# Two-layer token mixer and MLP on one core: x2 loaded between the halves of w1, tile 1 normalised before tile 2's statistics, tile 2 turned after tile 1's product

## The chip, the cores and the metric

The kernel runs on one NeuronCore of one Trainium2 chip. The metric is device time in microseconds (us) of one execution. The kernel before takes 135.35 us, the median of 3 runs (135.31 to 135.44).

## What is computed

All tensors are bfloat16; S = 2048 tokens, D = 512, F = 1792.

```python
h = gelu(layernorm(x) @ w1)                 # w1: 512 x 512
g0..g3 = the four 128-column quarters of h, shifted by +1, -1, +2, -2 tokens, zeros at the ends
x1 = x + concat(g0, g1, g2, g3) @ w2        # w2: 512 x 512
out = x1 + gelu(layernorm(x1) @ w3) @ w4    # w3: 512 x 1792, w4: 1792 x 512
```

`layernorm` subtracts the mean of a token's 512 values and divides by the square root of their variance plus 1e-5; it has no gain and no bias.

## The kernel before, in words

The tokens are cut into 16 tiles of 128. A tile of layer 1 passes these steps, each an operation with a name that carries the tile's number. The line is the one under which the profile lists it.

- `dma_x` (L384) loads x; `dma_w` (L393) loads a weight or half of one. All loads are issued by SP, on one queue, in the order of LOADS.
- Statistics: `bnst` and `bnag` on DVE (L432, L434), or, for the tiles in STAT_ACT (tile 0 among them), `sum` and `ssq` on ACT (L411, L416) followed by the small `msq` and `vpe` on DVE (L424, L428). `rstd` is a power of -0.5 on POOL (L439).
- `norm` (L461 on DVE) writes the normalised tile. Tile 0 is only centred (`norm0_0`, `norm0_1`, L448), and its factor `rstd0` is applied later.
- `tp` (L506) turns the tile on PE, in four 128x128 transposes into PSUM. `ev` (L514) copies the result to xnT in SBUF, on ACT, DVE, or half and half (`ev1act`, `ev1dve`).
- `up1:g` (L642) is the product with w1 in 128-column pieces, 16 matmuls for a group of one tile. Tile 0 uses `rows0` (L544) instead, with tokens as rows: four matmuls of 512 columns, then `gelur0` (L585, ACT, scaled by rstd0), then `th0` (L610, four transposes on PE) and `evh0` (L620, copy on DVE). For the other tiles `gelu1` (L657, ACT) writes h.
- `mix` (L697) is the shifted product with w2, four matmuls of 512 columns. mix0 needs h of tiles 0 and 1, so `evh0` and `gelu1` of tile 1. It is split in two halves. `x1` (L709, L713, DVE) adds x.

Layer 2 normalises x1 the same way, turns most tiles by DMA (L479), and multiplies by w3 (`up2`, L642) and w4 (`down`, L731). `res` (L739, DVE) adds x1, and an output DMA (L742) stores it.

Each engine carries out its own instructions strictly in their order in the program, and waits on semaphores for the results of other engines. PE's order is written out in SCRIPT: `sa`/`sb` are the halves of tile 0's transposes, `ty` a transpose, `ra`/`rb` the halves of rows0. The orders of the other four engines come from a planner (`order` and `place`, L54 to L273) that estimates durations and due times. The order that results for the first tiles is:

- SP: x0-1, x2, w1a, w1b, x3, x4-5, w2b, w2a, x6, ...
- DVE: bnst1, bnag1, norm0_0, norm0_1, bnst2, norm1, bnag2, msq0, vpe0, norm2, ev1dve, bnst3, ev2, bnag3, bnst4, evh0, norm3, ...
- ACT: sum0, ssq0, ev0_0, ev0_1, ev1act, gelur0, sum5, gelu1 of tile 1, ...
- POOL: rstd1, rstd2, rstd0, rstd3, ...
- PE: nine matmuls on zeros (L756), tp0, tp1, rows0, tp2, up1 of tile 1, th0, up1 of tile 2, mix0, tp3, mix1, ...

PSUM has three pairs of banks for `tp`, `rows0` and `up`, handed out in PE's order, one after the other in a ring, and two single banks for `mix`, `down` and `th0`.

Of the kernel before, what the change touches and what calls it, by code (L numbers as in the profile page):

```python
# [6 lines left out]
P = 128  # L7
# [7 lines left out]
class Op:  # L15


    def __init__(self, name, eng, fn, reads, writes, dur, queue):
        self.name, self.eng, self.fn = name, eng, fn
        self.reads, self.writes = list(reads), list(writes)  # L20
        self.dur, self.queue = dur, queue
        self.idx = 0
        self.descs = 8.0
        self.prio = 1e9
        self.first = None

class Program:

    HOP = {"pe": 200.0, "dve": 155.0, "act": 220.0, "pool": 120.0, "sp": 70.0}
    LOOK = {"dve": 300.0, "act": 300.0}
    DUE = 179877.0
    BEGIN = {"sp": 30.0, "act": 150.0, "pe": 400.0, "dve": 150.0, "pool": 450.0}
    ENTRY = 1900.0
    COLD, RESTART = 4300.0, 800.0
    RING = 150.0
    LAG = {"load": 750, "tp": 350}

    def __init__(self):  # L40
        self.ops = []
        self.lines = []

    def add(self, eng, name, fn, reads=(), writes=(), dur=100.0, queue=None):
        op = Op(name, eng, fn, reads, writes, dur, queue)
        op.idx = len(self.ops)
        self.ops.append(op)
        return op

    def line(self, names):  # L50

        self.lines.append(list(names))

    def order(self):  # L54
# [25 lines left out]
        order_only = set()  # L80
        for names in self.lines:
            for a, b in zip(names, names[1:]):
                assert named[a].eng == named[b].eng, (a, b)
                order_only.add((named[a].idx, named[b].idx))
        last = None
        pe_pos = 0
        for op in self.ops:
            if op.eng == "pe":
                if last is not None:
                    preds[op.idx].add(last.idx)  # L90
                last = op
                op.prio = pe_pos
                pe_pos += 1
        order_only = {(a, b) for a, b in order_only if a not in preds[b]}
        for a, b in order_only:
            preds[b].add(a)
        succs = [set() for _ in self.ops]
        for i, d in enumerate(preds):
            for j in d:
                succs[j].add(i)  # L100
        left = [len(s) for s in succs]
        stack = [i for i, n in enumerate(left) if n == 0]
        seen = 0
        while stack:
            i = stack.pop()
            seen += 1
            for j in preds[i]:
                if self.ops[j].eng != "pe":
                    self.ops[j].prio = min(self.ops[j].prio, self.ops[i].prio)
                left[j] -= 1  # L110
                if left[j] == 0:
                    stack.append(j)
        assert seen == len(self.ops), "cycle"
        if self.DUE:

            topo, left = [], [len(d) for d in preds]
            stack = [i for i, n in enumerate(left) if n == 0]
            while stack:
                i = stack.pop()
                topo.append(i)  # L120
                for j in succs[i]:
                    left[j] -= 1
                    if left[j] == 0:
                        stack.append(j)
            due, t = {}, self.DUE
            for op in self.ops:
                if op.eng == "pe" and not op.name.startswith("warm"):
                    due[op.idx] = t
                    t += op.dur
            for i in reversed(topo):  # L130
                op = self.ops[i]
                late = due.get(i, 1e9)
                for j in succs[i]:
                    o = self.ops[j]
                    hop = 70.0 if op.queue else (self.HOP[op.eng] if o.eng != op.eng else 120.0)
                    work = (2300.0 if op.queue == "tp" else op.dur + 1850.0) if op.queue else op.dur
                    late = min(late, o.prio - hop - work)
                op.prio = late
        for op in self.ops:
            op.prio += BIAS.get(op.name, 0.0)  # L140
            if op.first is not None:
                op.prio = op.first
        for names in self.lines:
            for a, b in reversed(list(zip(names, names[1:]))):
                named[a].prio = min(named[a].prio, named[b].prio - 1e-3)

        self.preds = preds
        out = self.place(succs, order_only)
        for a, b in order_only:
            preds[b].discard(a)  # L150
        return out

    def place(self, succs, order_only):

        npend = [len(d) for d in self.preds]
        ready = [0.0] * len(self.ops)
        cands = {e: [] for e in ENGINES}
        for op in self.ops:
            if npend[op.idx] == 0:
                cands[op.eng].append(op)  # L160
        free = dict(self.BEGIN)
        rings = {"sp": [], "act": []}
        fed = {}
        clock = moved = last = turned = self.total = 0.0
        out = []

        def finish(limit):
            nonlocal clock
            while True:
                heads = {e: r[0] for e, r in rings.items() if r}  # L170
                if not heads:
                    return None
                live = [e for e in heads if heads[e][0] <= clock]
                later = min([h[0] for h in heads.values() if h[0] > clock], default=1e18)
                if not live:
                    if later > limit:
                        return None
                    clock = later
                    continue
                first = min(live, key=lambda e: heads[e][1])  # L180
                step = heads[first][1] * len(live)
                ends = clock + step <= min(later, limit)
                if not ends:
                    step = min(later, limit) - clock
                for e in live:
                    heads[e][1] -= step / len(live)
                clock += step
                if ends:
                    return rings[first].pop(0)[2]
                if clock >= limit:  # L190
                    return None

        def release(op, o, at):
            npend[o.idx] -= 1
            if at is not None:
                ready[o.idx] = max(ready[o.idx], at)
            if npend[o.idx] == 0:
                cands[o.eng].append(o)

        def land(op):  # L200
            nonlocal moved, last, turned
            if op.queue == "tp":
                turned = max(clock + 500.0, op.start + 2450.0, last + 500.0, turned + 480.0)
                at = turned + self.LAG["tp"]
            elif op.name.startswith("out"):
                at = clock + 300.0
                self.total = max(self.total, at)
            else:
                moved += op.dur
                at = clock + 600.0 + min(600.0, 0.3 * moved) + (600.0 if op.dur > 1400.0 else 0.0)  # L210
                at += 50.0 if moved <= 1200.0 else self.LAG["load"] - 300.0 if moved <= 4000.0 else self.LAG["load"] if moved <= 11000.0 else self.LAG["load"] + 650.0
            if op.queue != "tp":
                last = max(last, at)
            op.landed = at
            for j in succs[op.idx]:
                if (op.idx, j) not in order_only:
                    release(op, self.ops[j], at + 30.0)

        while len(out) < len(self.ops):
            while True:  # L220
                best = None
                for e in ENGINES:
                    if cands[e]:
                        t = max(free[e], min(ready[o.idx] for o in cands[e]))
                        if best is None or t < best[0]:
                            best = (t, e)
                op = finish(best[0] if best else 1e17)
                if op is None:
                    break
                land(op)  # L230
            t, e = best
            look = self.LOOK.get(e, 1.0)
            op = min((o for o in cands[e] if ready[o.idx] <= t + look), key=lambda o: (o.prio, o.idx))
            cands[e].remove(op)
# [674 lines left out]
```

## Time and profile before

| what | value |
|---|---|
| median of 3 runs | 135.35 us (135.31 to 135.44) |
| span of the profiled execution, first to last instruction | 133.7 us |
| median less span | 1.65 us |
| busy DVE, ACT, POOL | 50.9, 56.0, 30.9 us |
| mean granted TensorE clock | 1.000 |
| DMA moved | 12.19 MB |

The page gives the profiled execution's span, but no time that includes what lies around it. The 1.65 us between the span and the median of the runs are taken as the same for both kernels. Times in a timeline count from the start of the span. A timeline line gives start, duration, engine, line, operation, what is written and read, and, in brackets, the idle time before it and what ended it. Several instructions of a kind may share one line (x4), and the duration then runs from the first one's start to the last one's end. Ends on PE are modelled, and an engine can start an instruction shortly before the end of the one before.

### The profile page before, as it was taken

What the parts mean: (1) busy time and instruction counts of PE and PEld (TensorE: products, weight loads), DVE (VectorE), ACT (ScalarE), POOL (GpSimd) and SP (SyncE); (2) the same over time, 40 slices, a digit from 0 to 9 for tenths busy, and PEclk for the clock granted to TensorE, in tenths of its full rate; (3) what the DMA queues carried; (4) which work ended last, traced back from release to release, by engine and by line L of the source; (5) the groups of instructions that cost most, each with busy time, mean ns of one, the idle gap of its engine ahead of it and who ended that gap; (6) DMA issues with size and microseconds to landing.
All of it is one profiled execution on the core that took longest, in us unless ns stands there. A gap on an engine that the chain in (4) does not pass through costs nothing.

```text
span 133.7 us, 2004 instructions
## 1 busy us (share of the span) xinstructions
PE 130.6 (98%) x776; PEld 71.8 (54%) x789; DVE 50.9 (38%) x138; ACT 56.0 (42%) x89; POOL 30.9 (23%) x69
## 2 busy tenths in 40 slices
PE   8999999999999999999999999999999999999994
PEld 3488768874488444444444444444444444444464
DVE  1899998887550830052260003322220000232223
ACT  5699998858657155520025553000006663000000
POOL 2447567696544120012022003100000000000000
PEclk9999999999999999999999999999999999999999
DMA  4999966745442991002211000311111000111112
GB/s 134 329 349 401 237 150 95 83 89 107 98 99 49 295 329 40 0 0 43 77 42 39 0 0 0 78 39 44 39 42 37 0 0 0 39 44 39 39 39 78
DMA packets 21305, 12.19 MB, mean 91 GB/s; under 512 B 13872, under 2 KB 20784, under 8 KB 21296
## 3 DMA queue, kind: packets, MB, share of 16 engines
q1 hardware_dynamic: 20864, 11.93, 32.7%
q10 hardware_dynamic: 432, 0.13, 0.4%
q8 instruction: 6, 0.10, 0.3%
q14 instruction: 3, 0.02, 0.1%
HBM read 6.82 MB, written 2.10 MB: 67 GB/s over the span
## 4 chain that ended last, share of the span: by engine, by line
PE 94%; DMA 2%; DVE 2%; issue 1%; SPq 0%
PE y_ps L642 46%; PE o_ps L731 36%; PE o_ps L697 10%; DMA x_sb<-in_x_dram 2%; PE y_ps L506 1%; DVE st L432 1%; PE y_ps L544 1%; DVE xn_buf L448 0%; DVE xn_buf L461 0%; DVE o_sb L739 0%; PE o_ps L610 0%; DVE mv L434 0%; SPq L894 0%
## 5 line engine op out<-in xcount | busy, mean ns | idle before, releaser
L642 PE MATMUL y_ps<-xnT,w_sb 128*128 128x512 bf16 (+2 forms) x421 | 63.6, 308 | 0.2
L642 PEld LDWEIGHTS y_ps<-xnT,w_sb 128*128 128x128 bf16 x424 | 38.4, 98 | 24.6 <-DVE mv L434 0.2
L731 PE MATMUL o_ps<-w_sb,h2T 128*128 128x512 bf16 (+3 forms) x248 | 48.7, 355 | 0.2
L657 ACT ACTIVATE h2T<-y_ps 128x1024 bf16<-128x1024 f32 (+1 forms) x29 | 28.6, 993 | 47.2 <-PE y_ps L642 47.1
L731 PEld LDWEIGHTS o_ps<-w_sb,h2T 128*128 128x128 bf16 x252 | 23.6, 98 | 25.2
L739 DVE TENSOR_TENSOR o_sb<-o_ps,x_sb 128x512 bf16<-128x512 f32 (+3 forms) x18 | 11.4, 632 | 45.7 <-PE o_ps L731 45.7
L439 POOL TENSOR_TENSOR rstd<-mv,neghalf 128x1 f32<-128x1 f32 x20 | 11.1, 553 | 35.1 <-DVE mv L434 30.1
L697 PE MATMUL o_ps<-w_sb,hT 128*128 128x512 bf16 x58 | 14.8, 379 | 0.3
L432 DVE BATCH_NORM_STATS2 st<-x_sb 128x6 f32<-128x512 bf16 x20 | 13.5, 676 | 2.6 <-DMA x_sb<-in_x_dram 2.5
L713 DVE TENSOR_TENSOR x_sb<-o_ps,x_sb 128x512 bf16<-128x512 f32 x10 | 6.8, 677 | 14.8 <-PE o_ps L697 14.8
L439 POOL TENSOR_TENSOR rstd<-vpe,neghalf 128x1 f32<-128x1 f32 x12 | 6.7, 558 | 15.6 <-DVE vpe L428 15.5
L473 POOL TENSOR_SCALAR xn_buf<-x_sb,rstd,nmr 128x512 bf16<-128x512 bf16 x12 | 9.2, 764 | 1.0 <-DVE nmr L466 0.4
L657 ACT ACTIVATE hT<-y_ps 128x512 bf16<-128x512 f32 (+1 forms) x10 | 8.1, 806 | 3.1 <-PE y_ps L642 2.9
L697 PEld LDWEIGHTS o_ps<-w_sb,hT 128*128 128x128 bf16 x64 | 6.1, 98 | 5.7
L709 DVE SCALAR_TENSOR_TENSOR x_sb<-o_ps,x_sb 128x512 bf16<-128x512 f32 x6 | 4.1, 681 | 12.1 <-PE o_ps L697 12.1
L416 ACT ACTIVATE junk<-x_sb 128x512 bf16<-128x512 bf16 x12 | 7.5, 622 | 2.1 <-DVE x_sb L709 2.0
L461 DVE TENSOR_SCALAR xn_buf<-x_sb,mv,rstd 128x512 bf16<-128x512 bf16 x13 | 6.1, 471 | 2.7 <-POOL rstd L439 2.0
L470 ACT ACTIVATE xn_buf<-x_sb,nmr,rstd 128x512 bf16<-128x512 bf16 x6 | 4.9, 813 | 0.5 <-POOL nmr L466 0.4
L756 PE MATMUL o_ps<-zeros 128*128 128x512 bf16 x9 | 4.0, 631 | 0.4 <-DVE zeros L363 0.4
L411 ACT ACTIVATE junk<-x_sb 128x512 bf16<-128x512 bf16 x6 | 3.7, 624 | 1.2 <-DMA x_sb<-in_x_dram 1.2
L434 DVE BATCH_NORM_AGGREGATE mv<-st 128x2 f32<-128x9 f32 x20 | 3.8, 192 | 0.3
L506 PE MATMUL y_ps<-ident,xn_buf 128*128 128x128 bf16 x32 | 3.4, 236 | 0.2 <-DVE xn_buf L461 0.2
(34 smaller groups left out, 28.7 us busy)
## 6 DMA issues: line engine op xcount, KB each, us to landing
out_dram<-o_sb SPq DMA_DIRECT2D x15, 128.0 KB, 1.7
w_sb<-in_w_dram SPq DMA_DIRECT2D x1, 1792.0 KB, 10.9
w_sb<-in_w_dram SPq DMA_DIRECT2D x2, 896.0 KB, 6.2
x_sb<-in_x_dram SPq DMA_DIRECT2D x4, 256.0 KB, 3.6
w_sb<-in_w_dram SPq DMA_DIRECT2D x4, 256.0 KB, 4.3
x_sb<-in_x_dram SPq DMA_DIRECT2D x5, 128.0 KB, 4.5
x_sb<-in_x_dram SPq DMA_DIRECT2D x1, 384.0 KB, 5.7
xnT<-xn_buf SPq DMA_TRANSPOSE x24, 2.5
```

The source lines that it names most:

```text
L416: (lambda d: (lambda e: e.activation(d, src, ACT_F.Square, accum_out=sums[:, q, 1:2])))(junk[:, b, :]),
L432: pg.add("dve", f"bnst{q}", lambda e: e.bn_stats(st9[:, q, 0:6], src), reads=rs, writes=[(("st", q), 0)], dur=605)
L439: lambda e: e.tensor_tensor(col(rstd), var, neghalf[:], ALU.pow),
L461: lambda e: e.tensor_scalar(dst, src, mv[:, q, 0:1], rstd[:, q : q + 1], ALU.subtract, ALU.mult),
L470: f = lambda e: e.activation(dst, src, ACT_F.Identity, bias=nmr[:, q : q + 1], scale=rstd[:, q : q + 1])
L473: f = lambda e: e.tensor_scalar(dst, src, rstd[:, q : q + 1], nmr[:, q : q + 1], ALU.mult, ALU.add)
L642: ins = e.matmul(y_ps[:, p, W * i : W * (i + 1)], wsb[:, dc, P * fc : P * (fc + 1)], src[:, dc, P * t0 : P * t0 + W], start=(dc == 0), sto ...
L657: (lambda d, s: (lambda e: e.activation(d, s, ACT_F.Gelu_apprx_tanh)))(dst, ysrc),
L697: ins = e.matmul(dst, hT[:, j, c0 : c0 + P], w2_sb[:, j, :], start=(j == order[0]), stop=(j == order[-1]))
L713: f = lambda e: e.tensor_tensor(x1_sb[:, t, :], dst, x_sb[:, t, :], ALU.add)
L731: ins = e.matmul(dst, h2T[:, fc, P * t : P * (t + 1)], w4_sb[:, fc, cs], start=(fc == 0), stop=(fc == FC - 1))
L739: (lambda d, c: (lambda e: e.tensor_tensor(o_sb[:, oi, c], d, x1_sb[:, t, c], ALU.add)))(dst, cs),
```

## The change

The planner is removed. The orders of SP, ACT, DVE and POOL stand in the program as lists (ORDER), and PE's order stays in SCRIPT. Set against the order of the kernel before, the lists differ in these places and nowhere else:

1. SP: dma_w1a stands ahead of dma_x2, so x2 lies between w1a and w1b.
2. DVE: norm1 stands ahead of bnst2.
3. DVE: ev1dve stands ahead of norm2.
4. PE: tp2 (`ty:2`) stands behind up1 of tile 1. As PSUM pairs are handed out in PE's order, tp2 and this up1 exchange their pairs.

The instructions themselves are the same, as are the 15 operations that stand ahead of the start barrier (AHEAD). EVAC, NMR and HEV lose entries that no operation used.

```diff
 LOADS = """
-x0-1 x2 tp2 w1a w1b x3 x4-5 w2b w2a tp5 x6 tp6 x7 x8-10 tp4 w3 x12-13 tp0 x11 tp17 x14-15 tp26 tp5 w4a tp3
-w4b
+x0-1 w1a x2 w1b x3 x4-5 w2b w2a x6 x7 x8-10 w3 x12-13 x11 x14-15 w4a w4b
 """
 SCRIPT = """
-warm:9 sa:0 sb:0 ty:1 ra:0 rb:0 ty:2 up1:1 th:0 up1:2 mix:0 ty:3 mix:1 ty:4 up1:3 ty:5 up1:4 ty:6 mix:2
+warm:9 sa:0 sb:0 ty:1 ra:0 rb:0 up1:1 ty:2 th:0 up1:2 mix:0 ty:3 mix:1 ty:4 up1:3 ty:5 up1:4 ty:6 mix:2 up1:5
...
+ORDER = {
+    "sp": """
+dma_x0 dma_w1a dma_x2 dma_w1b dma_x3 dma_x4 dma_w2b dma_w2a dma_x6 dma_x7 dma_x8 dma_w3 dma_x12 dma_x11 tp16
...
+    "act": """
+warm_gelu sum0 ssq0 ev0_0 ev0_1 ev1act gelur0 sum5 gelu1_1_0 ssq5 gelu1_2_0 sum7 ev3 norm5 ssq7 gelu1_3_0 sum9
...
+    "dve": """
+zeros bnst1 bnag1 norm0_0 norm0_1 norm1 bnst2 bnag2 msq0 vpe0 ev1dve norm2 bnst3 ev2 bnag3 bnst4 evh0 norm3
...
+    "pool": """
+trip0 trip1 neghalf ident0 epsc pad0 ident1 pad1 rstd1 rstd2 rstd0 rstd3 rstd4 rstd5 nmr5 rstd6 nmr6 norm6
...
+        lists = {e: [named[n] for n in ORDER[e].split()] for e in ENGINES if e != "pe"}
+        lists["pe"] = [op for op in self.ops if op.eng == "pe"]
...
+            heads = [lists[e][at[e]] for e in ENGINES if at[e] < len(lists[e])]
+            heads = [op for op in heads if preds[op.idx] <= done]
+            op = min(heads, key=lambda op: (op.name not in AHEAD, ENGINES.index(op.eng)))
```

## The prediction

> **What bounds the kernel now.** I read the page first, for the engine that sets the end, then the chain of waits for the place where it starts to do so, then the timelines of DVE, PE and POOL over the first 9 us. PE is busy for nearly the whole span, and the chain is almost all PE:
>
> ```profile
> PE 130.6 (98%) x776; PEld 71.8 (54%) x789; DVE 50.9 (38%) x138; ACT 56.0 (42%) x89; POOL 30.9 (23%) x69
> ```
>
> In time order the chain enters PE for good at 5.12 us. The two pieces just ahead of that are tile 2's statistics (bnst2) and, queued behind them on DVE, tile 1's normalisation (norm1):
>
> ```profile
> 4.15 0.60 DVE st L432
> 4.75 0.33 DVE xn_buf L461
> ```
>
> PE's timeline shows the packed train that follows (tp0, tp1, rows0, tp2, up1 of tile 1, th0, up1 of tile 2):
>
> ```profile
> 4.24 0.63 PE L506 MATMUL y_ps<-ident,xn_buf 128*128 128x128 bf16 x4
> 5.12 0.49 PE L506 MATMUL y_ps<-ident,xn_buf 128*128 128x128 bf16 x4 [0.25 <-DVE xn_buf L461]
> 5.45 1.03 PE L544 MATMUL y_ps<-w_sb,xnT 128*128 128x512 bf16 x4
> 6.32 0.39 PE L506 MATMUL y_ps<-ident,xn_buf 128*128 128x128 bf16 x4
> 6.54 1.06 PE L642 MATMUL y_ps<-xnT,w_sb 128*128 128x128 bf16 x16
> 7.43 0.39 PE L610 MATMUL o_ps<-ident,hn 128*128 128x128 bf16 x4
> 7.66 1.06 PE L642 MATMUL y_ps<-xnT,w_sb 128*128 128x128 bf16 x16
> ```
>
> Read the starts: four transposes every 0.22 us, 16 small matmuls every 0.89, four wide ones every 0.87. From 5.45 each group starts where the last one's pace ends, so PE has no hole. mix0 follows at 7.66 + 0.89 = 8.55; the first of its records is missing, and the chain's "issue" pieces of 0.05 us are such gaps. After that PE only works, up to 131.9. So **the time moves by as much as mix0 moves**, provided nothing stalls later. Its inputs come from DVE:
>
> ```profile
> 4.07 0.68 DVE L432 BATCH_NORM_STATS2 st<-x_sb 128x6 f32<-128x512 bf16 x1
> 4.67 0.39 DVE L461 TENSOR_SCALAR xn_buf<-x_sb,mv,rstd 128x512 bf16<-128x512 bf16 x1
> 4.99 0.18 DVE L434 BATCH_NORM_AGGREGATE mv<-st 128x2 f32<-128x9 f32 x1
> 5.09 0.17 DVE L424 TENSOR_SCALAR mv<-mv 128x1 f32<-128x1 f32 x1
> 5.29 0.16 DVE L428 SCALAR_TENSOR_TENSOR vpe<-sums,mv 128x1 f32<-128x1 f32 x1
> 5.84 0.41 DVE L461 TENSOR_SCALAR xn_buf<-x_sb,mv,rstd 128x512 bf16<-128x512 bf16 x1 [0.39 <-POOL rstd L439]
> 6.17 0.28 DVE L514 COPY xnT<-y_ps 128x256 bf16<-128x256 bf16 x1
> 6.37 0.69 DVE L432 BATCH_NORM_STATS2 st<-x_sb 128x6 f32<-128x512 bf16 x1
> 6.97 0.41 DVE L514 COPY xnT<-y_ps 128x512 bf16<-128x512 bf16 x1
> 7.29 0.19 DVE L434 BATCH_NORM_AGGREGATE mv<-st 128x2 f32<-128x9 f32 x1
> 7.39 0.65 DVE L432 BATCH_NORM_STATS2 st<-x_sb 128x6 f32<-128x512 bf16 x1
> 7.96 0.41 DVE L620 COPY hT<-o_ps 128x512 bf16<-128x512 bf16 x1
> ```
>
> These are bnst2, norm1, bnag2, msq0, vpe0, norm2, ev1dve, bnst3, ev2, bnag3, bnst4 and evh0. DVE is nearly full, and evh0 ends at 8.37, only 0.18 before mix0 starts. POOL has the two powers between them, rstd2 and rstd0:
>
> ```profile
> 5.25 0.55 POOL L439 TENSOR_TENSOR rstd<-mv,neghalf 128x1 f32<-128x1 f32 x1 [0.81 <-DVE mv L424]
> 5.77 0.55 POOL L439 TENSOR_TENSOR rstd<-vpe,neghalf 128x1 f32<-128x1 f32 x1
> ```
>
> **Hand-over times**, all from these rows. A DVE instruction that needs nothing new starts 0.08 before the end of the one before (4.67 against 4.75), and one that needs its result 0.03 behind that end (5.26 to 5.29). POOL to DVE 0.04 (5.80 to 5.84), DVE to POOL 0.08 (5.17 to 5.25), DVE to PE 0.06 (5.06 to 5.12), PE to a reader 0.04. The second of two powers starts 0.52 behind the first. A transpose's result stands 0.22 behind its start.
>
> **The loads (edit 1).** By the list of DMA issues, x2 is issued at 0.59 and lands 2.6 us later, at about 3.15; w1a 1.08 + 3.7, at about 4.75; w1b at about 5.5. In the new order w1a lands no later than now, and w1b has the same bytes ahead. That is worth nothing: rows0's first half is paced by PE to 5.45, 0.7 behind w1a, and its second half starts at 5.89, 0.37 behind w1b. x2 in third place is not in the trace. It lands at 3.15 at best (its present place), at 5.52 at worst (w1b's place). I take at most 4.75, when the three first transfers, the same 640 KB, have all landed now. DVE comes to x2 at 4.79, so the move costs nothing. Beyond 4.77 it costs its full lateness.
>
> **The start (edit 2).** rstd1 (POOL, 3.88 for 0.56) is done at 4.44; norm1 no longer sits behind bnst2 and runs 4.48 to 4.87, and tp1 starts at 4.93 instead of 5.12: 0.19 earlier. Part is lost at once. tp0's four starts lie 0.107 apart, twice the later 0.056; the pace of tp1 changes in its course, at about 5.37. At that time still, tp1 takes 0.40 instead of 0.33 and rows0 starts at 5.33 (now 5.45). PE is free for the next group at 6.21.
>
> **What waits (edits 2 and 3).** bnst2 now starts at 4.87 - 0.08 = 4.79 instead of 4.07 and ends at 5.47. bnag2 5.50 to 5.69, msq0 5.61 to 5.77, vpe0 5.81 to 5.97, ev1dve (moved up) 5.89 to 6.17. up1 of tile 1 starts at 6.17 + 0.06 = 6.23, 0.02 behind PE's being free, where tp2 started at 6.32 before. So up to here 0.09 is won.
>
> **What is turned late (edit 4).** up1 runs its 0.89 to 7.12, and tp2 takes 7.12 to 7.34. norm2 is long done: rstd2 5.77 to 6.33, norm2 6.36 to 6.78. But three things now stand behind this:
>
> - th0 needs gelur0, which needs rstd0: 5.77 + 0.52 = 6.29, done at 6.84 (now 6.32). With some 0.08 to ACT (a row for it is missing; 0.04 as to DVE, 0.14 as the nearest ACT instruction behind POOL, at 10.44) and 0.69 for itself, gelur0 ends at 7.61 and th0 starts at 7.67. PE idles 0.33.
> - ev2 needs tp2's result at 7.12 + 0.39 = 7.51. It runs 7.55 to 7.96, 0.58 later than now, while DVE idles about 0.25 behind bnst3 (6.70 to 7.38). up1 of tile 2 starts at 8.02 instead of 7.66.
> - bnag3, bnst4 and evh0 are queued behind ev2 on DVE: 7.88, 7.98 and 8.55. evh0 ends at 8.96, and mix0 starts at 9.02 instead of 8.55. th0's result (about 8.06) isn't the last to come, so ACT's unknown 0.04 to 0.14 is covered by 0.5 us.
>
> **The sum.** 9.02 - 8.55 = 0.47; without rounding the rows 0.45. I take 0.45. As holes on PE: 0.19 fewer ahead of tp1, 0.09 lost to the slow pace, then 0.02 + 0.33 + 0.13 + 0.11 new ones ahead of up1, th0, up1 of tile 2 and mix0. Behind mix0 all is as before but later: DVE lags 0.55 and PE 0.45, and the spare 0.1 is there: norm3 is ready 0.7 ahead of tp3, norm4 0.3 ahead of tp4, and ACT's copies and GELUs, the nearest with 0.1 to spare, wait for PE and move with it. The exchanged PSUM pairs add no wait: the pair of up1 was read out by 5.36, tp2's by 6.17. Span 133.7 + 0.45 = 134.15; with the 1.65 us around it, 135.80. What this measurement can tell from no change is about 0.2%, 0.27 us.
>
> **Rivals.**
>
> - *x2 lands late in the new place* (0.08). At w1b's 5.52, bnst2 starts at 5.54, everything behind it 0.75 later: 136.55. Against it: DMA moved only about 240 GB/s from 2 to 4 us, and 375 in the next; there is room to land sooner.
> - *Faster: the timed runs have x2 later than the profiled one* (0.08). Now norm1 stands behind bnst2, which waits for x2; every us past 4.05 delays the present kernel one for one and the new one not before 4.77. It turns at a landing of 4.50. At w1a's 4.75 the present kernel would lose 0.70, and the new one would be 0.25 below it: 135.10. Against it: x2 landed at 3.15, and three runs agree within 0.13 us.
> - *Within 0.2%* (0.10). The path from rstd1 to mix0 has a dozen hand-overs; at 0.015 less each the loss is 0.27: 135.62.
> - *The fast pace of PE comes later* (0.06). The place is rows0. If it came only at 5.89, where rows0's second half starts now, rows0 from 5.33 on would lose half of 0.56, 0.26 more than counted, and up1, tp2, ev2 and mix0 0.24: 136.04. The present kernel would lose half of 0.44 too, so it decides only where the two kernels differ in it; three runs within 0.13 speak against. [...]
> - *The lists change nothing* (0.02): 135.35. The four places are plain in them.
>
> **How the numbers follow.** The forecast has 0.66. Slower by over 0.2%: 0.66 + 0.08 + 0.06 = 0.80. Within: 0.10 + 0.02 = 0.12. Faster: 0.08. The range, 135.6 to 136.2, leaves out the faster case, no change, the later half of the late x2 (from 5.2 on) and some of the near-equal case, together just under 0.2.
>
> **What would show it.** Right: norm1 near 4.48, bnst2 near 4.79 with no wait for its load, up1 of tile 1 near 6.23, idle PE ahead of th0 (0.3) and mix0 (0.1), ev2 near 7.55 waiting for PE, mix0 near 9.0, no holes later. Wrong: bnst2 waiting for x2; th0 with no idle time; evh0 ending before 8.6.

## The result and the profile after

The changed kernel takes 135.95 us, the median of 13 runs (135.68 to 136.24); the kernel before, beside it, 135.35 (135.14 to 136.04). The ratio is 1.0037, with a 95% interval of 1.0025 to 1.0048: slower by 0.50 us (0.34 to 0.65); the medians lie 0.60 apart. The profiled execution took 136.01 with a span of 134.7. Ratios are those of the fast runs alone: in loads_only, act_x2_early and w1_whole, below, one run each, at 137.43 to 137.52, is left out as slow.

In the lines after, the line numbers are new: `tp` is L340, `rows0` L377, `up` L473, `th0` L442, `mix` L527, `bnst` L267, `norm` L295, `ev` L348, `evh0` L452, `down` L561, `res` L569. The page of the kernel after:

```profile
PE 131.3 (97%) x789; PEld 71.4 (53%) x789; DVE 51.2 (38%) x138; ACT 56.3 (42%) x89; POOL 30.9 (23%) x69
```

PE's work is the same, in a span 1.0 us longer (its 131.3 us against 130.6 come with 13 more of its records in the trace). Its chain of waits, in order of time (start, duration, what), with pieces left out:

```profile
1.58 4.63 DMA w_sb<-in_w_dram
...
8.02 0.44 DVE xnT L348
8.46 0.04 issue
8.50 1.07 PE y_ps L473 x16
...
132.91 0.26 DVE o_sb L569
```

Two things are new in the chain: the load of w1b, which ends at 6.22, and ev2 (L348), which PE waits for ahead of up1 of tile 2. From mix0 on nothing has changed: mix0 to the last `res` is 131.96 - 8.55 = 123.41 us before and 132.91 - 9.50 = 123.41 after. So the whole difference arises ahead of mix0. PE's timeline there:

```profile
4.21 0.39 PE L340 MATMUL y_ps<-ident,xn_buf 128*128 128x128 bf16 x4
5.05 0.40 PE L340 MATMUL y_ps<-ident,xn_buf 128*128 128x128 bf16 x4 [0.45 <-DVE xn_buf L295]
5.29 0.59 PE L377 MATMUL y_ps<-w_sb,xnT 128*128 128x512 bf16 x2
6.26 0.60 PE L377 MATMUL y_ps<-w_sb,xnT 128*128 128x512 bf16 x2 [0.38 <-DMA w_sb<-in_w_dram]
6.70 1.06 PE L473 MATMUL y_ps<-xnT,w_sb 128*128 128x128 bf16 x16
7.60 0.39 PE L340 MATMUL y_ps<-ident,xn_buf 128*128 128x128 bf16 x4
7.82 0.39 PE L442 MATMUL o_ps<-ident,hn 128*128 128x128 bf16 x4
8.50 1.07 PE L473 MATMUL y_ps<-xnT,w_sb 128*128 128x128 bf16 x16 [0.30 <-DVE xnT L348]
9.50 1.04 PE L527 MATMUL o_ps<-w_sb,hT 128*128 128x512 bf16 x4
```

The order is tp0, tp1, the halves of rows0, up1 of tile 1, tp2, th0, up1 of tile 2, mix0. Where the train had no hole before, there are three now, by the pace of the starts: 0.54 between the halves of rows0 (6.26 less 5.29 + 0.43), 0.46 ahead of up1 of tile 2 (8.50 less 7.82 + 0.22), and 0.11 ahead of mix0 (9.50 less 8.50 + 0.89). Each bracket counts a hole from the modelled end of the last matmul and so shows less. DVE's timeline:

```profile
4.58 0.41 DVE L295 TENSOR_SCALAR xn_buf<-x_sb,mv,rstd 128x512 bf16<-128x512 bf16 x1 [0.32 <-POOL rstd L274]
4.91 0.69 DVE L267 BATCH_NORM_STATS2 st<-x_sb 128x6 f32<-128x512 bf16 x1
...
6.03 0.28 DVE L348 COPY xnT<-y_ps 128x256 bf16<-128x256 bf16 x1
...
8.02 0.42 DVE L348 COPY xnT<-y_ps 128x512 bf16<-128x512 bf16 x1 [0.51 <-PE y_ps L340]
...
9.03 0.41 DVE L452 COPY hT<-o_ps 128x512 bf16<-128x512 bf16 x1
```

These are norm1, bnst2, ev1dve, ev2 and evh0. x0-1 landed 0.11 later in this execution (bnst1 starts at 2.98, not 2.87). With that taken off, the first three stand at 4.47, 4.80 and 5.92; the forecast had 4.48, 4.79 and 5.89. ev2 waits for PE, as forecast, but at 8.02 instead of 7.55 + 0.11, as up1 of tile 1 started at 6.70 instead of 6.23 + 0.11. evh0 ends at 9.44, 0.06 ahead of mix0.

**Two theories.** *Queue theory*, that of the prediction: tile 2's statistics come 0.7 us later on DVE, so tp2, ev2 and, queued behind ev2, evh0 and mix0 come later. *Load theory*: with x2 between the halves of w1, w1b lands late, and rows0 waits for it. The profile after shows both at once.

### The profile page after: what moved, and what is told of

Same layout as the page of the kernel before. It is cut to its first block, busy times and chain, and to the rows that moved or that the text cites. A ratio compares the mean times of both kernels' runs of the same rounds, so it can differ in the third digit from the quotient of the medians.

```text
span 134.7 us, 2017 instructions
## 1 busy us (share of the span) xinstructions
PE 131.3 (97%) x789; PEld 71.4 (53%) x789; DVE 51.2 (38%) x138; ACT 56.3 (42%) x89; POOL 30.9 (23%) x69
## 4 chain that ended last, share of the span: by engine, by line
PE 94%; DMA 3%; SPq 1%; DVE 1%; issue 0%
PE y_ps L473 46%; PE o_ps L561 36%; PE o_ps L527 10%; DMA w_sb<-in_w_dram 3%; PE y_ps L340 1%; SPq L220 1%; PE y_ps L377 0%; SPq L229 0%; DVE xnT L348 0%; DVE o_sb L569 0%; SPq L711 0%
## 5 line engine op out<-in xcount | busy, mean ns | idle before, releaser
L473 PE MATMUL y_ps<-xnT,w_sb 128*128 128x512 bf16 (+2 forms) x424 | 63.8, 309 | 0.3 <-DVE xnT L348 0.3
L473 PEld LDWEIGHTS y_ps<-xnT,w_sb 128*128 128x128 bf16 x424 | 38.4, 98 | 25.3 <-DVE xnT L348 0.5
L561 PE MATMUL o_ps<-w_sb,h2T 128*128 128x512 bf16 (+3 forms) x252 | 48.9, 355 | 0.0
L561 PEld LDWEIGHTS o_ps<-w_sb,h2T 128*128 128x128 bf16 x252 | 23.6, 98 | 25.2
L569 DVE TENSOR_TENSOR o_sb<-o_ps,x_sb 128x512 bf16<-128x512 f32 (+3 forms) x18 | 11.4, 632 | 45.8 <-PE o_ps L561 45.8
L527 PE MATMUL o_ps<-w_sb,hT 128*128 128x512 bf16 x64 | 15.8, 379 | 0.0
L267 DVE BATCH_NORM_STATS2 st<-x_sb 128x6 f32<-128x512 bf16 x20 | 13.5, 675 | 2.7 <-DMA x_sb<-in_x_dram 2.6
L527 PEld LDWEIGHTS o_ps<-w_sb,hT 128*128 128x128 bf16 x64 | 6.0, 98 | 5.8
L295 DVE TENSOR_SCALAR xn_buf<-x_sb,mv,rstd 128x512 bf16<-128x512 bf16 x13 | 6.1, 472 | 2.8 <-POOL rstd L274 2.1
L300 POOL TENSOR_SCALAR nmr<-mv,rstd 128x1 f32<-128x1 f32 x13 | 3.4, 263 | 0.8
```

The lines of the kernel that those rows point to most:

```text
L267: pg.add("dve", f"bnst{q}", lambda e: e.bn_stats(st9[:, q, 0:6], src), reads=rs, writes=[(("st", q), 0)])
L295: lambda e: e.tensor_scalar(dst, src, mv[:, q, 0:1], rstd[:, q : q + 1], ALU.subtract, ALU.mult),
L473: ins = e.matmul(y_ps[:, p, W * i : W * (i + 1)], wsb[:, dc, P * fc : P * (fc + 1)], src[:, dc, P * t0 : P * t0 + W], start=(dc == 0), sto ...
L527: ins = e.matmul(dst, hT[:, j, c0 : c0 + P], w2_sb[:, j, :], start=(j == order[0]), stop=(j == order[-1]))
L561: ins = e.matmul(dst, h2T[:, fc, P * t : P * (t + 1)], w4_sb[:, fc, cs], start=(fc == 0), stop=(fc == FC - 1))
L569: (lambda d, c: (lambda e: e.tensor_tensor(o_sb[:, oi, c], d, x1_sb[:, t, c], ALU.add)))(dst, cs),
```

## Experiments

Each ratio is to the kernel before, timed beside it on the same chip. As the loads land at other times in every execution, the profiles are compared from the start of bnst1 (x0-1 has landed) to the start of mix0. Where the first of mix0's records is missing, its start is taken 0.22 ahead of the first one shown.

| kernel | ratio (95%) | bnst1 | mix0 | between | x2 lands | w1b lands |
|---|---|---|---|---|---|---|
| before | 1 | 2.87 | 8.55 | 5.68 | 3.15 | 5.52 |
| after | 1.0037 (1.0025 to 1.0048) | 2.98 | 9.50 | 6.52 | 4.53 | 6.22 |
| undo_all | 1.0001 (0.9983 to 1.0020) | 2.94 | 9.61 | 6.67 | 3.21 | 6.89 |
| loads_only | 1.0022 (1.0003 to 1.0042) | 2.96 | 9.07 | 6.11 | 4.56 | 5.24 |
| no_loads | 1.0025 (1.0009 to 1.0041) | 2.95 | 9.22 | 6.27 | 3.26 | 5.79 |
| turn_back | 1.0029 (1.0009 to 1.0049) | 2.88 | 9.10 | 6.22 | 4.36 | 5.68 |
| after_again | 1.0014 (0.9996 to 1.0033) | 2.80 | 9.19 | 6.39 | 4.11 | 5.91 |
| evh0_up | 1.0039 (1.0018 to 1.0059) | 3.05 | 9.14 | 6.09 | 4.77 | 5.55 |
| half_after | 1.0006 (0.9987 to 1.0024) | 2.93 | 8.96 | 6.03 | 4.57 | 5.42 |
| half_turn | 1.0008 (0.9988 to 1.0028) | 2.83 | 9.35 | 6.52 | 5.29 | 6.00 |

### undo_all: all four moves undone, orders still as lists

```diff
-dma_x0 dma_w1a dma_x2 dma_w1b dma_x3
+dma_x0 dma_x2 dma_w1a dma_w1b dma_x3
-norm0_1 norm1 bnst2 bnag2 msq0 vpe0 ev1dve norm2 bnst3
+norm0_1 bnst2 norm1 bnag2 msq0 vpe0 norm2 ev1dve bnst3
-up1:1 ty:2 th:0
+ty:2 up1:1 th:0
```

> All four moves undone, with the orders still given as lists. Two theories for the loss of 0.5 to 0.6 us. Queue theory: tile 2's statistics come 0.7 us later on DVE, so tp2, ev2 and, queued behind ev2, evh0 and mix0 come some 0.45 later. Load theory: with x2 between the halves of w1, w1b lands late (6.22 us after the start in the profiled run, 5.52 before), and the second half of rows0 waits for it. Both expect no change from the kernel before here (within 0.2%), PE without a hole from about 5.45, and w1b landing near 5.5. A third reading, that the lists themselves cost time, expects 0.3% to 0.5% more than before.

The ratio is 1.0001 (0.9983 to 1.0020): within 0.2% the lists cost nothing, and the moves hold the loss. But the profiled execution has the largest hole of all in rows0, with the loads in the old order, which neither theory expected (PE's timeline):

```profile
6.94 0.60 PE L377 MATMUL y_ps<-w_sb,xnT 128*128 128x512 bf16 x2 [0.91 <-DMA w_sb<-in_w_dram]
```

w1b landed at 6.89 instead of near 5.5. So a late w1b is no work of move 1; it comes with the old order too.

### loads_only: move 1 alone

```diff
-norm0_1 norm1 bnst2 bnag2 msq0 vpe0 ev1dve norm2 bnst3
+norm0_1 bnst2 norm1 bnag2 msq0 vpe0 norm2 ev1dve bnst3
-up1:1 ty:2 th:0
+ty:2 up1:1 th:0
```

> Move 1 alone: w1a ahead of x2, everything else as before. norm1 stands behind bnst2 again, and bnst2 has to wait for x2, which landed at 4.53 in the profile after: bnst2 near 4.55 instead of 4.07. Queue theory: everything from norm1 on is 0.45 to 0.5 late, ratio near 1.0035, and the second half of rows0, now due near 6.36, no longer waits for w1b at 6.22. Load theory: the loss is there too, 0.35 to 0.5, but with a hole between the two halves of rows0.

Measured 1.0022 (1.0003 to 1.0042), where 1.0035 was expected, and 0.43 more from bnst1 to mix0 in the profile. DVE's timeline shows bnst2 waiting for x2, norm1 behind it at 5.19 instead of 4.67, and rows0 had no hole (w1b at 5.24), as the queue theory has it:

```profile
4.58 0.69 DVE L267 BATCH_NORM_STATS2 st<-x_sb 128x6 f32<-128x512 bf16 x1 [0.35 <-DMA x_sb<-in_x_dram]
5.19 0.40 DVE L295 TENSOR_SCALAR xn_buf<-x_sb,mv,rstd 128x512 bf16<-128x512 bf16 x1
```

### no_loads: moves 2, 3 and 4, loads in the old order

```diff
-dma_x0 dma_w1a dma_x2 dma_w1b dma_x3
+dma_x0 dma_x2 dma_w1a dma_w1b dma_x3
```

> Moves 2, 3 and 4 with the loads as in the kernel before (x2 ahead of both halves of w1). Queue theory: the loss stays, 0.45 us, ratio 1.0033, with up1 of tile 1 near 6.23, ev2 near 7.55 and mix0 near 9.0. Load theory: w1b lands near 5.5 again, rows0 has no hole, and the loss goes: within 0.2% of before or faster.

The loss stays, 1.0025, and its interval leaves out 1. DVE's timeline has ev2 at 7.74, waiting for PE:

```profile
7.74 0.42 DVE L348 COPY xnT<-y_ps 128x512 bf16<-128x512 bf16 x1 [0.27 <-PE y_ps L340]
```

As the cause of the loss, the load theory falls with this run and undo_all: the loss is there without move 1, and the late w1b is there without the change. What is left of it is that a late w1b can add to the time of single executions.

### turn_back: moves 1, 2 and 3, tp2 ahead of up1 of tile 1 again

```diff
-up1:1 ty:2 th:0
+ty:2 up1:1 th:0
```

> Moves 1, 2 and 3, with tp2 back ahead of up1 of tile 1. Queue theory: PE now waits for norm2 ahead of tp2 (norm2 ends near 6.78, tp2 near 6.83), up1 of tile 1 follows at 7.05, and mix0 comes near 9.05: 0.49 us more than before, so within 0.1 us of the changed kernel; move 4 neither loses nor wins here. Load theory: rows0 still waits for w1b, the loss of the changed kernel stays; a loss well below it would say that move 4 is what costs.

1.0029 (1.0009 to 1.0049), within the noise of the changed kernel. PE now waits for norm2 ahead of tp2 (its timeline):

```profile
6.87 0.40 PE L340 MATMUL y_ps<-ident,xn_buf 128*128 128x128 bf16 x4 [0.54 <-DVE xn_buf L295]
```

tp2 was expected near 6.83. Move 4 exchanges a hole ahead of tp2 for one ahead of up1 of tile 2. In this profile another 0.38 is lost behind the start of mix0, to late loads: w2a landed at 9.65 and held the second half of mix0 by 0.16, and a load of x issued at 4.59 landed at 10.39 and held ACT's statistics, the copy queued behind them and so up1 of tile 3 by 0.22. So the 6.22 of the table doesn't hold all of this execution's loss.

### after_again, evh0_up, half_after, half_turn

after_again is the changed kernel once more.

> The changed kernel once more, for a second profile and as the partner of the next three. Queue theory: ratio 1.003 to 1.005; where w1b lands before 5.7, rows0 is whole, up1 of tile 1 starts near 6.3, ev2 waits for PE, mix0 comes at 9.0 to 9.2. Load theory: w1b lands late again, near 6.2, and the hole of 0.4 us in rows0 is there in this execution too.

1.0014 (0.9996 to 1.0033), below the expected 1.003 to 1.005, less than the 1.0037 of the first measurement and not clear of no change by itself; the two intervals overlap. In its profile w1b landed at 5.91, outside the case expected for a whole rows0, and held rows0 there by 0.29; up1 of tile 1 started at 6.40, 0.22 later than ev1dve (done at 6.12) would have let it.

evh0_up, on the changed kernel:

```diff
-ev2 bnag3 bnst4 evh0 norm3
+ev2 evh0 bnag3 bnst4 norm3
```

> The changed kernel with evh0 directly behind ev2 on DVE, ahead of bnag3 and bnst4. Queue theory: evh0 comes 0.66 earlier, mix0 is paced by PE again and follows up1 of tile 2 without a hole; 0.1 us less than the changed kernel, 0.35 more than before. If bnag3 and bnst4 ahead of evh0 cost nothing, the hole ahead of mix0 stays and so does the time.

The hole ahead of mix0 went, as expected: up1 of tile 2 at 8.24, plus 0.89, gives 9.13, and mix0 starts there (its second matmul is the first one shown, at 9.36). The gain in time did not come: 1.0039 (1.0018 to 1.0059), against 1.0014 for after_again beside it; the intervals overlap. PE's timeline shows where it went:

```profile
8.24 1.07 PE L473 MATMUL y_ps<-xnT,w_sb 128*128 128x128 bf16 x16
9.36 0.81 PE L527 MATMUL o_ps<-w_sb,hT 128*128 128x512 bf16 x3
...
10.23 1.03 PE L527 MATMUL o_ps<-w_sb,hT 128*128 128x512 bf16 x4
11.29 0.40 PE L340 MATMUL y_ps<-ident,xn_buf 128*128 128x128 bf16 x4
```

mix1 starts at 10.23 and takes 0.86, but tp4 starts at 11.29 instead of 11.09, 0.06 behind the end of norm4; two smaller holes of 0.12 and 0.06 follow up to 13.7. Tile 4's statistics were moved back, and with them norm4, which tp4 needs. DVE has next to no idle time in this stretch (from ev2 at 7.76 to bnst6 at 10.23 its timeline shows one wait, of 0.17, ahead of norm3), so moving its work about moves the hole.

half_after, on the changed kernel:

```diff
-lambda e: e.bn_stats(st9[:, q, 0:6], src)
+lambda e: e.bn_stats(st9[:, q, 0:6], src[:, 0 : D // 2] if q == 2 else src)
```

> The changed kernel with bnst2 over 256 of the 512 columns, so tile 2 is normalised by the statistics of half its columns; bnst2 takes about 0.35 instead of 0.69. Queue theory: vpe0, rstd0, gelur0 and th0 come 0.33 earlier, and the hole ahead of th0 goes; but up1 of tile 1 can't start before PE is free, tp2 stays behind it, and ev2, evh0 and mix0 stay within 0.05 us: no gain over the changed kernel. The rival, that the late statistics themselves are the cost, expects 0.33 less, ratio to before near 1.001.

1.0006 (0.9987 to 1.0024), not told apart from after_again's 1.0014 by time. In the profile, bnst1 to mix0 takes 6.03 instead of 5.68, so 0.35 of the loss stays even so. bnst2 took 0.42 instead of 0.69, not the 0.35 expected. By this profile the expectation of no gain was too strict: the fast pace of PE came at about 5.2, PE was free at 6.17, and up1 of tile 1 started there; with a full bnst2 ev1dve would have held it to about 6.3. So the wait for ev1dve can be some 0.15 of the loss, an estimate, where PE gets through rows0 early.

half_turn has the same edit and tp2 back ahead of up1 of tile 1.

> The same half bnst2 (tile 2 normalised by half its columns) with tp2 back ahead of up1 of tile 1. Queue theory: with this order the late statistics are the cost: norm2, tp2 (near 6.5), up1 (6.73) and mix0 (8.73) come 0.3 earlier than with tp2 turned back alone, 0.18 us more than before, ratio 1.0013. The rival expects about the same time as the other kernel with half bnst2.

1.0008 (0.9988 to 1.0028), where turn_back had 1.0029 in another measurement, on another chip: by ratio a gain of about 0.3 us, as expected, but the intervals overlap, so the gain isn't shown. The profile can't confirm it, since x2 landed at 5.29 in that execution, 0.5 later than DVE came to it (its timeline):

```profile
5.31 0.43 DVE L267 BATCH_NORM_STATS2 st<-x_sb 128x6 f32<-128x256 bf16 x1 [0.48 <-DMA x_sb<-in_x_dram]
```

This is the rival "x2 lands late in the new place" caught in one execution. half_turn and half_after are not told apart by time.

### Loads from a second queue: act_x2_late, act_x2_early, w1_whole, moves_act

As w1b's landing held rows0 in several profiles, four kernels load in other ways. Three of them have moves 2 to 4 undone, and moves_act keeps these moves (the lists of loads are changed to match):

```diff
# act_x2_late and moves_act: x2 is issued by ACT
-dma_x0 dma_w1a dma_x2 dma_w1b dma_x3
+dma_x0 dma_w1a dma_w1b dma_x3
-warm_gelu sum0 ssq0
+warm_gelu dma_x2 sum0 ssq0
# act_x2_early: the same, but
+dma_x2 warm_gelu sum0 ssq0
# w1_whole: x2 ahead, w1 in one DMA
-dma_x0 dma_w1a dma_x2 dma_w1b dma_x3
+dma_x0 dma_x2 dma_w1 dma_x3
```

> Moves 2 to 4 undone; x2 is issued by ACT, behind its first small GELU, so that SP issues w1a and w1b half a microsecond earlier. Late-load theory: the kernel before is often held in rows0 by the last part of w1b, which landed anywhere from 5.2 to 6.9 in the profiles so far; with w1b issued near 1.1 it lands before 5.5, and x2 before 4.1, so PE has no hole and the median falls by 0.2 to 0.3 us (ratio 0.998). Rival: the lateness is that of single DMA rings, whatever the time of issue: no change, or slower where x2 comes after 4.1.

> The same with x2 issued by ACT as its first instruction, about 0.2 us after the start, beside x0-1. Late-load theory: w1b lands before 5.5, but x0-1 shares the DMA engines with x2 and may land 0.1 to 0.3 later, which delays everything one for one: between 0.2 us faster and 0.1 slower than before. Rival (single rings late whatever the time of issue): the hole in rows0 stays, slower by what x0 loses.

> Moves 2 to 4 undone, x2 ahead of w1 as before, and w1 loaded by one DMA of 512 KB instead of two of 256 KB. Late-load theory: one issue less, all of w1 lands near 5.2, rows0 waits for it as a whole but the later loads come 0.5 earlier: within 0.2% of before, with fewer late cases. Rival: rows0's first half now waits for the slowest ring of the whole, 0.2 to 0.5 us slower.

> Moves 2, 3 and 4 of the change with x2 issued by ACT and w1a, w1b earlier from SP. Queue theory: rows0 is whole, up1 of tile 1 near 6.25, the holes ahead of th0, up1 of tile 2 and mix0 stay, and mix0 comes near 9.0: 0.45 us more than the same loads with the old orders, whatever that kernel gives. Load theory: no more than those.

None beats the kernel before. w1_whole: 1.0019 (1.0000 to 1.0039); all of w1 landed at 5.89. act_x2_early: 1.0046 (1.0010 to 1.0082); w1b landed at 4.92, PE had no hole, and from bnst1 to mix0 it took 5.68 again, but x0-1, with x2 issued beside it, landed 0.4 later (3.26 against 2.85), more than expected. Eight of its twelve runs took 135.45 to 136.00 and four 137.35 to 137.52, which is what lifts its ratio; there is no profile of one of the four, so their cause is open. act_x2_late: 1.0182 (1.0144 to 1.0221), 138.3 us, where 0.998 was expected: x2, issued by ACT at 1.17, landed only at 5.97, behind w1a (3.65) and beside w1b (6.24). In its profile PE waits for norm1, which stands behind bnst2, which waits for x2:

```profile
7.06 0.61 PE L340 MATMUL y_ps<-ident,xn_buf 128*128 128x128 bf16 x4 [2.47 <-DVE xn_buf L295]
7.46 1.91 PE L377 MATMUL y_ps<-w_sb,xnT 128*128 128x512 bf16 x4
```

moves_act has the same loads with moves 2 to 4: 1.0064 (1.0041 to 1.0086), 136.47 us. x2 landed at 5.77 in its profile, yet tp1 started near 5.0. The queue theory expected 0.45 more than act_x2_late; it got 1.8 us less. The expectation missed, as it took x2 to land before 4.1. With x2 landing where it did, this is the prediction's rival "faster", made to happen: once x2 lands after about 4.5, the old order pays its lateness in full on the way to tp1, and the new one doesn't. In moves_act a late x2 shows only from up1 of tile 1 on. Most of the 1.8 us is a consequence of the second order: after its long wait PE ran at half pace from 7.06 to 10.02 in act_x2_late (shown below), which is worth half of 2.96, some 1.5 us. The rest, about 0.3, is the direct effect; by the prediction's terms, with x2 at 5.97 and 5.77, it would be 5.97 - 4.05 - 0.45 - (5.77 - 4.77) = 0.47. The runs bear this out: four of the five of act_x2_late have a mean granted clock of 0.988 and took 138.06 to 138.50, and the fifth, with a clock of 1.000, took 136.96, 1.4 less than the median of the four and 0.49 above moves_act.

The late-load theory gets no support. With w1b issued half a microsecond sooner, at 1.08 or 1.09, it landed at 4.92, 5.59 and 6.24 in the three kernels that did so: it comes sooner or later from one execution to the next all the same, as the rival had it. That single rings are the reason isn't shown.

## Why the prediction was right

It said slower, 135.80 us, a ratio of 1.0033; measured were 135.95 and 1.0037 (1.0025 to 1.0048). By its steps:

- **The end moves with mix0.** Right: 123.41 us from there to the last `res` in both. Ahead of it the two profiles differ by more than forecast: bnst1 to mix0 takes 6.52 instead of 5.68, 0.84 more, where the prediction has 0.47 (its list of holes adds up to 0.49).
- **The start (norm1, tp1).** Right in size: norm1 0.20 earlier, tp1 at 5.05 less the 0.11 of x0-1, 4.94 against 4.93. The 0.09 lost to the slow pace depends on the execution: in the one after, tp0 already ran at the fast pace (0.39 for four, 0.63 before), while in no_loads the change came near 5.7. It decides little where up1 waits for ev1dve or w1b anyway.
- **bnst2, ev1dve.** Right within 0.03.
- **th0.** A hole of 0.33 was forecast. It was 0 in the profile after, where w1b had held up1 and tp2 longer than rstd0, 0.05 in after_again, 0.18 in no_loads and 0.26 in evh0_up. The prediction named a th0 without idle time as a sign of being wrong; in the profile after it is w1b that took the place of this wait. gelur0 started 0.03 behind rstd0 (6.98 to 7.01), at the low end of the 0.04 to 0.14 taken. As forecast, this hole isn't what mix0 waits for.
- **ev2 behind PE, evh0 behind ev2.** Right: ev2 waits for tp2 in after, no_loads, after_again and evh0_up, and moving evh0 up closes the hole ahead of mix0. What the prediction left out is that closing it this way wins nothing.
- **The loads.** "It costs nothing" holds beside moves 2 to 4, as with them move 1 neither makes the loss nor removes it. By itself it costs 0.22% (loads_only), as bnst2 then waits for x2 with norm1 behind it. And w1b was taken to land at 5.5 in every execution; it came between 5.24 and 6.89 in the ten profiles above, and in the profile after it held up1 to 6.70, where ev1dve, done at 6.31, would have let it start at 6.37: 0.33 of the 0.84, which belongs to the execution and not to the change.
- **What lies around the span.** 1.65 us was wrong: by the run after it is 136.01 - 134.7 = 1.31. So the profiled execution of before stands for some 133.7 + 1.31 = 135.0 us, below all its timed runs (135.14 at the least): w1b came early enough in it to hold nothing. In five of the ten profiles of the table w1b held rows0, by 0.1 to 1.1, so a typical execution seems to have some wait for a load in it; for the timed runs this isn't shown. The sum 135.80 is the forecast difference put on the median, with such waits inside the 1.65. That they would weigh about the same in both kernels was not argued: here the prediction had luck. A hint that 0.45 is about right without them: the fastest runs lie 0.54 apart in the first measurement (135.68 and 135.14) and 0.43 in that of after_again (135.49 and 135.06).

What stays open: the size of the loss to better than a tenth of a per cent (1.0037 and 1.0014 for the same kernel in two measurements); how moves 2 and 3 share it, as neither was made alone and the kernels with half of bnst2 are not told apart from theirs with the whole by time; and why the last part of a load comes late in some executions.

## What to carry to other kernels

Where one engine works without a hole, find the last input that comes just in time (here evh0, 0.12 us ahead of need), and follow the whole in-order queue that feeds it (in loads_only norm1, behind a waiting bnst2, came at 5.19 instead of 4.67): moving one instruction up by 0.2 us can put a 0.7 us instruction in front of everything else. Where that queue is full, a reorder may only choose where the hole appears, as evh0_up did here, so compare the holes of all orders before one is chosen. One profile is one execution: take what the loads do in several before a wait on a load is called hidden.

## What the runs showed of the hardware

A 256 KB load issued at the same time landed up to 1.65 us apart in different executions: w1b between 5.24 and 6.89 in the ten profiles of the table, issued between 1.56 and 1.60 in all. The completions of its 16 parts stand within 0.57 us in the kernel before (4.95 to 5.52) and are spread over 1.75 in the one after (4.46 to 6.22, the last one 0.52 behind the one before it).

A second queue brought x2 no clear gain. x2, issued by ACT at 1.17, landed at 5.97 in act_x2_late and 5.77 in moves_act; on SP's queue, issued at 1.08 between the halves of w1, it came at 4.11 to 5.29. The place in line isn't the same, as both halves of w1 had been issued ahead of it in the first two. Issued by ACT at 0.21, beside x0-1 (act_x2_early), it landed at 3.08; second on SP's queue, issued at 0.59 in the kernel before, at 3.15.

Behind an idle time of 2.47 us PE ran at half pace: in the profile of act_x2_late rows0 took 0.43 a matmul instead of 0.22. Here the granted clock shows it; the view by stretch of time gives the stretch, its length, the busy time of five engines with instructions, granted clock, DMA share and GB/s:

```profile
6.00:7.00 1.00, 0.00 (x0) 0.00 (x0) 1.00 (x3) 0.00 (x0) 0.00 (x0) 0.81 1.12 348
7.00:8.00 1.00, 0.94 (x6) 0.67 (x7) 0.58 (x5) 0.29 (x1) 0.81 (x2) 0.50 1.02 300
...
10.00:11.00 1.00, 1.00 (x21) 1.00 (x19) 0.93 (x3) 0.88 (x4) 0.55 (x1) 0.99 1.04 419
```

With the clock taken as whole or half, as in the stretches between (0.50), 0.81 in the stretch from 6 puts the start of the half clock at 6.62 (0.38 at a half), and 0.99 in the one from 10 its end at 10.02: 3.40 us, an estimate from these shares. PE's last transpose ahead of the wait ended at 4.59 (4.20 + 0.39), so the clock fell some 2.03 us into the wait, and it came back some 2.96 us after PE had started again at 7.06. In the fifth run of act_x2_late, with a clock of 1.000, it seems not to have fallen at all. The start of the fast pace at the beginning of the program moves as well: before 4.21 us in the kernel after, at 5.37 in the one before and about 5.7 in no_loads, the last two estimates from the spacing of the matmuls; PE is at work from 0.43 in the kernel before and from 0.44 in the one after. The granted clock doesn't show that: it is 1.00 in each stretch from 0 to 6 of both kernels, while tp0's starts lie 0.107 apart in the one before and 0.058 in the one after. What sets these times isn't shown.
